# The last 64 positions of each sequence: loaded through another engine's queue, and in 9 transfers where there were 12

## The chip, the cores and the metric

The kernel runs on one core of a Trainium2 chip. A core has five engines that each work through their own list of instructions in order: TensorE (PE in the profile, with its weight loads as PEld), VectorE (DVE), ScalarE (ACT), GpSimd (POOL) and SyncE (SP). They meet only at semaphores. Sixteen DMA engines move data between the large memory and the on-chip buffers; the transfers of this kernel are issued by SyncE, and a few small ones by ScalarE. The metric is the device time of one launch in microseconds, the median of several runs.

## The reference

Two blocks follow each other, all in float32.

- Retention: q, k and v have the shape (8 batches, 8 heads, 576 positions, 64). For each batch and head the scores q·kᵀ/8 are multiplied by a causal decay, gamma_h to the power of the distance, with gamma_h = 1 − 2^(−5−h), and then multiplied with v. There is no softmax.
- The result is laid out as 4608 tokens by 512 and goes through an RMS norm with a gain, and a gated feed-forward block: silu(xn·w_gate) · (xn·w_val), and that times w_out. w_gate and w_val are 512 by 1536, w_out is 1536 by 512.

```
ret = scale * (q @ k.T) * Dmat;  x = (ret @ v) laid out as (4608, 512)
xn = x / sqrt(mean(x*x) + 1e-6) * rms_g
out = (silu(xn @ w_gate) * (xn @ w_val)) @ w_out
```

## The kernel before

**Tiling.** One job is a batch and a pair of heads; there are 32. The first 8 jobs (batches 0 and 1) are worked on in a start phase that also rounds the weights and builds sums of their blocks; the rest is one long run of matmuls on blocks of 512 tokens, in which the later jobs are placed. A sequence of 576 positions is 4 full chunks of 128 and a tail of 64. The full chunks of a job are loaded by `load_first` (line 165): one transfer for q (256 KB), two for k and two for v (128 KB each). The tails are loaded by `load_tails` (line 184), for several heads of one batch at a time, with one transfer each for q, k and v, into the tile `vi`.

**A job in the start phase.** `scale_v` (line 268, step V of the plan) multiplies v and its tail by powers of gamma, four small instructions of ScalarE. `turn` (line 222, step T) transposes q and k on TensorE, the tails too, and ScalarE copies the results out of PSUM, which gives qT and kT. `slot` (line 414, step S) then does `values` of the job before, `scores` and `states` of this one, `weigh` and `sums` on VectorE, and `carried` of the job before.

**What sets the order.** Each engine's order is the order in which the program issues work; nothing is rearranged. In `start` (line 1206) ScalarE first gets the load of its function table and one dummy activation, then three table loads (`gv`, `causal`, `gc`, line 1220). After that the list `LOADS` (line 1155) is gone through once: it holds everything that SyncE loads in this phase, in order: tails and jobs, the table `gq`, and the first halves of the weights (`load_half`, line 1031). Then the string `PLAN` (line 1134) is gone through, one step after the other; it begins with `V0 T0 a1 a1 a1 S0 T1 V1 a1 S1 T2 V2`. The tails are four entries of `LOADS` with three transfers each: heads 0 and 1 of batch 0 at the head of the list, heads 2 to 7 of batch 0 and heads 0 and 1 of batch 1 behind job 1, heads 2 to 7 of batch 1 behind job 4.

**Semaphores of the transfers.** The framework gives all transfers of SyncE and ScalarE together eight semaphores, in rotation, in the order in which it lays the transfers out. A transfer waits, in the list of the engine that issues it, until the transfer eight places before it, which had the same semaphore, has landed. So at most eight are under way. Before the change the only transfers of ScalarE are the three tables.

Of the kernel before, what the change touches and what calls it, by code (L numbers as in the profile page):

```python
# [23 lines left out]
def _decay_tables(H, D):  # L24

    pairs = _gamma(H).reshape(H // 2, 2).T
    rows = np.repeat(pairs, D, axis=0)
    pos = np.arange(L)  # L30
    p = np.concatenate([pos, pos])
    gq = rows[:, :, None] ** (pos + L) / np.sqrt(D)
    turns = np.arange(2)[None, None] * SQ + (np.arange(P) % SQ)[:, None, None] + L
    gp = rows[:, :, None] ** turns / np.sqrt(D)
    t = pairs.T[None] ** -p[:, None, None], rows**L, gq, gp
    return [np.ascontiguousarray(x).astype(np.float32) for x in t]


def _causal_table():

    return np.ascontiguousarray(np.tile(np.triu(np.ones((L, L), np.float32)), (2, 1)))
# [3 lines left out]
def kernel(  # L45
# [11 lines left out]
    nc = tc.nc  # L57
    B, H, S, D = q.shape
# [58 lines left out]
    rms_g = const.tile([P, NHP], F32, name="rms_g")  # L117
# [66 lines left out]
    def load_tails(b, heads):  # L184

        for n, (nm, src) in enumerate((("qt", q), ("kt", k), ("vt", v))):
            at = NV + (3 * b + n) * DM
            t = vi[:TAIL, at : at + DM].rearrange("p (h d) -> p h d", d=D)
            cut = slice(heads[0], heads[-1] + 1)
            nc.sync.dma_start(  # L190
                out=t[:, cut], in_=src[b, cut, NFULL * P :].rearrange("h p d -> p h d")
            )
            for hp in range(heads[0] // 2, heads[-1] // 2 + 1):
                st[b * NHP + hp][nm] = t[:, 2 * hp : 2 * hp + 2]
# [17 lines left out]
    def warm_up(n, width=P):  # L212

        if not warm_of:
            warm_of[0] = bank("warm")
        for _ in range(n):
            nc.tensor.matmul(
                warm_of[0][:, :width], lhsT=ones, rhs=ones[:, :1].to_broadcast([P, width]),
                start=True, stop=True,
            )  # L220
# [193 lines left out]
    def slot(j, rest=True):  # L414

        if rest:
            values(j - 1)
        scores(j)
        states(j)
        weigh(j)  # L420
        if j < FIRST:
            sums(j)
        if rest:
            carried(j - 1)
        if j >= FIRST:
            sums(j)
# [17 lines left out]
    def squared(u, c):  # L444
        return u, c, square(u, c)

    def gather(u, c, sq):

        if c == NHP - 1 and u > 1:
            nc.vector.scalar_tensor_tensor(  # L450
                out=sq, in0=t_of[u], scalar=EPS * DM / P, in1=sq, op0=ALU.add, op1=ALU.add
            )
        elif u < 2 and c == NHP - 1:
            sq = (t_of[u], sq)
        elif c:
            nc.vector.tensor_tensor(out=sq, in0=t_of[u], in1=sq, op=ALU.add)
        t_of[u] = sq
# [245 lines left out]
    def differences(u, f):  # L703

        hh = h_1 if u == 1 else h
        b11, b12, b22 = hh[:, f : f + 2, :HU], hh[:, f : f + 2, HU:], hh[:, NH + f : NH + f + 2, HU:]
        for o, a, b in ((t1_of(u)[:, f : f + 2], b12, b11), (b12, b22, b12)):
            nc.vector.tensor_tensor(out=o, in0=a, in1=b, op=ALU.subtract)
# [30 lines left out]
    def inner_sums(u, n, part=None, eng=nc.gpsimd):  # L739

        x = operands_of(u)[order_of(u)[n]]
        x11, x12 = x[:, :NK, :P], x[:, :NK, P:]
        x21, x22 = x[:, NK:, :P], x[:, NK:, P:]
        i1, i3, i2, i4 = inner_of(u, n)
        if part != 1:
            eng.tensor_tensor(out=i1, in0=x12, in1=x11, op=ALU.subtract)  # L746
        c = slice(1, NK) if part == 1 else slice(0, 1) if part == 0 else slice(0, NK)
        for o, a, b, op in (
            (i3, x22, x12, ALU.subtract), (i2, i3, x11, ALU.add), (i4, x21, i2, ALU.subtract),
        ):  # L750
            eng.tensor_tensor(out=o[:, c], in0=a[:, c], in1=b[:, c], op=op)  # L751
# [227 lines left out]
    def combine(b, eng=nc.vector, late=False):  # L979

        t = vec[:, b] if isinstance(b, slice) else vec[:, b : b + 1]
        for o, x, y in (
            (A12, A11, A12), (A11, A11, S2), (S1, A11, S1), (S4, S1, S4), (A11, A11, S3),
            (S3, S1, S3), (A22, A11, A22),
        ):
            eng.tensor_tensor(out=t[:, :, o], in0=t[:, :, x], in1=t[:, :, y], op=ALU.add)  # L986
        if late:
            store(NU - 1, b)
# [42 lines left out]
    def load_half(i, queue):  # L1031
        if i >= len(halves):
            return
        kind, k, a, c = halves[i]
        w = words_of(i)
        if kind == "up":
            src = (moe_w_gate, moe_w_val)[k % 2].bitcast(U32)
            n = (a * NH + k // 2 * 2) * P * 2
            src = src[2 * c * P : 2 * c * P + 2 * P, n : n + 4 * P].rearrange("(c p) f -> p c f", p=P)
            w = w.rearrange("p (c f) -> p c f", c=2)  # L1040
        else:
            f = (a * NH + c * NK + k) * P
            src = moe_w_out.bitcast(U32)[f : f + P]
        queue.dma_start(out=w, in_=src)
# [82 lines left out]
    def store_blocks(n):  # L1127

        while stores and stores[0][0] <= n:
            for o, t in stores.pop(0)[1]:  # L1130
                nc.sync.dma_start(out=o, in_=t)
# [19 lines left out]
        c0 F13 A1 v1 A1 c3 A1 j9 o0 G11 A1 A1 j10 A1 A1 j11 A1 i12 A1 R2 A1 Y2 A1 X2 M2 a1 a1  # L1151
        i13 A1 A1 A1 A1
    """
    TAILS = ((0, range(2)), (0, range(2, H)), (1, range(2)), (1, range(2, H)))
    LOADS = [("tails", 0), ("job", 0), ("job", 1), ("tails", 1), ("tails", 2), ("job", 2), ("table", 3), ("job", 3), ("half", 0), ("half", 1), ("job", 4), ("tails", 3), ("job", 5), ("job", 6), ("job", 7), ("half", 2), ("half", 3), ("rms_g", 0), ("table", 4), ("half", 4)]
    stores = []
    n_joined = 0
    due = False
# [47 lines left out]
    def start():  # L1206

        tables = list(zip((causal, gv, gc, gq, gp), (_causal_table(), *_decay_tables(H, D))))

        def table(i, queue):  # L1210
            t, values_ = tables[i]
            src = nc.inline_tensor(values_, name=t.tensor.name + "_table")
            queue.dma_start(out=t, in_=src.ap())

        make_identity(nc, ident)
        nc.scalar.activation(out=tick, in_=mhalf[:1], func=AF.Silu)
        nc.vector.memset(ones, 1.0)
        warm_up(6)
        for i in (1, 0, 2):
            table(i, nc.scalar)  # L1220
        squares, outs = [], [across(0), across(1)]
        loads = {
            "job": load_first, "table": lambda i: table(i, nc.sync),
            "half": lambda i: load_half(i, nc.sync),
            "tails": lambda i: load_tails(*TAILS[i]),
            "rms_g": lambda i: nc.sync.dma_start(
                out=rms_g, in_=moe_rms_g.rearrange("(c p) -> p c", p=P)
            ),
        }
        tasks = {  # L1230
            "S": lambda j: slot(j, rest=j not in (0, FIRST)), "C": close, "T": turn, "V": scale_v,
            "P": prepare, "F": fetch, "Q": lambda j: squares.append(squared(*divmod(j, NHP))),
            "G": lambda j: gather(*squares.pop(0)), "N": norm_1, "D": diagonals, "X": norm_2,
            "w": weights, "a": act, "d": lambda f: differences(f // 3, 2 * (f % 3)),
            "i": lambda n: inner_sums(*divmod(n, 7)),
            "j": lambda n: inner_sums(*divmod(n, 7), eng=nc.vector),
            "c": lambda b: combine(b, nc.gpsimd), "v": combine,
            "b": lambda n: (second_operand, last_operand)[n % 2](n // 2),
            "z": lambda n: store_blocks(len(halves) + 9),
            "r": refill, "W": weights_to, "A": lambda u: next(outs[u], None), "R": root_1,  # L1240
            "Y": root_2, "M": sums_of_x, "o": store,
            "k": lambda _: nc.vector.tensor_scalar(
                out=rms_k, in0=rms_g, scalar1=3.0 / 8.0 * K1, scalar2=None, op0=ALU.mult
            ), "U": lambda n: up_plain(n // 100, n // 10 % 10, n % 10),
        }
        for what, i in LOADS:
            loads[what](i)
        for step in PLAN.split():
            tasks[step[0]](int(step[1:]))

    with tc.manual_schedule():
        start()
        for u in range(2, NU):
            j0 = NHP * (u + 1)
# [60 lines left out]
```

## Time and profile before

| | |
|---|---|
| median of 3 runs | 1108.38 us (1107.13 to 1108.67) |
| the profiled execution | 1109.0 us, of which the profile's span covers 1107.2 us |
| busy share of the span | PE 98%, DVE 68%, POOL 41%, ACT 30% |
| the chain that ended last, by engine | PE 94%, DVE 2%, the rest 1% or less each |
| first step of the plan on ScalarE (V0) | begins at 8.14 us |
| first scores on TensorE (S0) | begin at 10.52 us |
| first transfer of job 0 | issued by SyncE at 2.87 us, after three transfers of tails |

Times are counted from the first instruction of the span. "SPq" and "ACTq" are the engines' sequencers, which issue transfers; their rows begin when the waits of that transfer are over. A chain row names what the end waited for, stretch by stretch. "Issue" is time in which an engine waited for nothing that the profile shows.

### The profile page before, as it was taken

How to read it: one execution, taken by the hardware profiler on the slowest of the kernel's cores; microseconds unless marked ns; L12 is line 12 of the kernel's file. 1: busy time of each engine (PE TensorE's matmuls, PEld its weight loads, DVE VectorE, ACT ScalarE, POOL GpSimd, SP SyncE). 2: the span in 40 equal slices, each digit the busy share in tenths (PEclk: the TensorE clock that was granted, in tenths of full speed). 3: DMA queues.
4: the chain of work that ended last, by engine and by line, in shares of the span. 5: the costliest groups of instructions: out<-in, count | busy, mean ns of one | idle time of the engine just before them, and what ended most of it. 6: DMA issues, size and time to landing. Idle time of an engine off the chain costs nothing.

```text
span 1107.2 us, 24479 instructions
## 1 busy us (share of the span) xinstructions
PE 1089.9 (98%) x10102; PEld 914.2 (83%) x10102; DVE 755.3 (68%) x1243; ACT 337.5 (30%) x749; POOL 458.5 (41%) x421
## 2 busy tenths in 40 slices
PE   7899999999999999999999999999999999999998
PEld 6654444479988899889988998889888998898888
DVE  4888578777866685668667775669465935594466
ACT  5745475331123411333034303331233111211110
POOL 0025335538430286026802481239311942393236
PEclk9999999999999999999999999999999999999999
DMA  8756787596878876787768865978475755585471
GB/s 203 204 174 222 262 266 218 198 339 190 288 269 225 197 262 218 207 234 231 261 197 208 284 253 160 247 232 286 146 206 199 268 200 172 183 289 162 151 249 40
DMA packets 253872, 243.60 MB, mean 220 GB/s; under 512 B 193217, under 2 KB 213825, under 8 KB 247617
## 3 DMA queue, kind: packets, MB, share of 16 engines
q1 hardware_dynamic: 252752, 241.74, 69.4%
q8 instruction: 79, 1.29, 0.5%
q10 hardware_dynamic: 1008, 0.30, 0.1%
q14 instruction: 33, 0.26, 0.1%
HBM read 211.92 MB, written 30.08 MB: 219 GB/s over the span
## 4 chain that ended last, share of the span: by engine, by line
PE 94%; DVE 2%; SPq 1%; issue 1%; DMA 1%; ACT 1%; POOL 0%; POOLq 0%; ACTq 0%; DVEq 0%
PE up L684 15%; PE x L624 13%; PE w L624 13%; PE z L624 13%; PE y L624 7%; PE xo L789 6%; PE xp L789 4%; PE zo L789 4%; PE zp L789 3%; PE yo L789 2%; PE wo L789 2%; PE av L362 2%; PE av L382 2%; PE s L292 2%; PE yp L789 2%; PE wp L789 2%
## 5 line engine op out<-in xcount | busy, mean ns | idle before, releaser
L684 PE MATMUL up<-x,ring 128*128 128x512 f32 x384 | 166.8, 594 | 0.0
L624 PE MATMUL x<-x,ring 128*128 128x256 f32 x672 | 161.0, 382 | 0.0
L624 PE MATMUL w<-sums,ring 128*128 128x256 f32 x672 | 158.9, 379 | 0.0
L624 PE MATMUL z<-x,ring 128*128 128x256 f32 x672 | 158.7, 379 | 0.0
L746 POOL TENSOR_TENSOR vi<-h 128x384 f32<-128x384 f32 x32 | 39.5, 1234 | 276.5 <-DVE h L643 267.5
L684 PEld LDWEIGHTS up<-x,ring 128*128 128x128 f32 x384 | 72.4, 190 | 88.9 <-issue 84.9
L624 PEld LDWEIGHTS z<-x,ring 128*128 128x128 f32 x672 | 127.7, 190 | 19.9 <-issue 2.9
L624 PEld LDWEIGHTS w<-sums,ring 128*128 128x128 f32 x672 | 127.6, 190 | 17.4
L624 PEld LDWEIGHTS x<-x,ring 128*128 128x128 f32 x672 | 125.4, 190 | 17.3
L751 POOL TENSOR_TENSOR vi<-h 128x384 f32<-128x384 f32 (+2 forms) x46 | 46.5, 1011 | 149.3 <-DVE h L643 149.3
L986 POOL TENSOR_TENSOR vi<-vi 128x512 f32<-128x512 f32 (+1 forms) x77 | 78.2, 1028 | 38.6 <-DVE vi L816 33.2
L624 PE MATMUL y<-sums,ring 128*128 128x256 f32 x336 | 79.4, 379 | 1.5 <-DVE sums L543 1.5
L650 ACT COPY m<-x 128x512 f32<-128x512 f32 x42 | 24.6, 586 | 174.0 <-PE x L624 174.0
L631 DVE TENSOR_TENSOR h<-u,w 128x512 f32<-128x512 f32 x42 | 28.9, 688 | 68.3 <-PE w L624 68.3
L624 PEld LDWEIGHTS y<-sums,ring 128*128 128x128 f32 x336 | 63.8, 190 | 10.5 <-issue 1.8
L631 DVE TENSOR_TENSOR u<-m,y 128x512 f32<-128x512 f32 x42 | 28.9, 688 | 63.2 <-PE y L624 62.9
L645 ACT ACTIVATE h<-h 128x512 f32<-128x512 f32 x63 | 39.7, 630 | 84.5 <-DVE h L631 84.5
L341 DVE SCALAR_TENSOR_TENSOR sum<-sum,gc,s 128x64 f32<-128x64 f32 x192 | 53.9, 281 | 6.8
L1106 POOL TENSOR_TENSOR vi<-vi 128x512 f32<-128x512 f32 (+1 forms) x24 | 40.8, 1699 | 36.8 <-DVE vi L1095 14.6
L631 DVE TENSOR_TENSOR u<-u,z 128x512 f32<-128x512 f32 x42 | 28.9, 688 | 34.7 <-PE z L624 34.7
L751 POOL TENSOR_TENSOR vi<-vi,h 128x384 f32<-128x384 f32 (+2 forms) x46 | 48.1, 1046 | 3.6
L1106 POOL TENSOR_TENSOR ring<-ring 128x512 f32<-128x512 f32 x24 | 30.6, 1278 | 42.0 <-DVE ring L1095 34.9
(311 smaller groups left out, 2068.1 us busy)
## 6 DMA issues: line engine op xcount, KB each, us to landing
ring<-w_out_blocks SPq DMA_DIRECT2D x59, 1344.0 KB, 6.6
ring<-w_up_blocks SPq DMA_DIRECT2D x42, 1792.0 KB, 7.8
w_out_blocks<-vi SPq DMA_DIRECT2D x21, 448.0 KB, 5.8
out_dram<-vi SPq DMA_DIRECT2D x64, 128.0 KB, 3.0
qraw<-in_q_dram SPq DMA_DIRECT2D x96, 72.0 KB, 4.7
kraw<-in_k_dram SPq DMA_DIRECT2D x96, 72.0 KB, 2.6
k<-in_k_dram SPq DMA_DIRECT2D x48, 128.0 KB, 2.9
v<-in_v_dram SPq DMA_DIRECT2D x48, 128.0 KB, 2.8
```

The source lines that it names most:

```text
L292: nc.tensor.matmul(s[e][side(odd), i * L : i * L + L], lhsT=d["kT"][side(e), c * L : c * L + L], rhs=d["qT"][side(e), c * L : c * L + L], ...
L341: nc.vector.scalar_tensor_tensor(out=t[:, c], in0=t[:, c - 1], scalar=gc[:, hp : hp + 1], in1=part, op0=ALU.mult, op1=ALU.add,)
L624: nc.tensor.matmul(ps[:, i * HU : i * HU + HU], lhsT=w[:, PLACE[blk], c, i * P : i * P + P], rhs=t_of[u][blk][:, c], start=(start and i == ...
L631: nc.vector.tensor_tensor(out=o, in0=a, in1=pairs_of(ps), op=ALU.add)
L645: nc.scalar.activation(out=o, in_=c, func=AF.Silu)
L650: nc.scalar.copy(out=s1, in_=pairs_of(x_))
L684: nc.tensor.matmul(ps, lhsT=w[:, PLACE[blk], c % 2, i * P : i * P + P], rhs=x_of[u][:, c], start=(c == 0), stop=(c == NHP - 1),)
L746: eng.tensor_tensor(out=i1, in0=x12, in1=x11, op=ALU.subtract)
L751: eng.tensor_tensor(out=o[:, c], in0=a[:, c], in1=b[:, c], op=op)
L789: nc.tensor.matmul(ps, lhsT=lhs[:, c], rhs=w[:, s, c], start=((nm, s // 4) not in first), stop=False, skip_group_check=True,)
L986: eng.tensor_tensor(out=t[:, :, o], in0=t[:, :, x], in1=t[:, :, y], op=ALU.add)
L1106: nc.gpsimd.tensor_tensor(out=t[o], in0=t[x], in1=t[y], op=op)
```

## The change

`load_tails` issues on ScalarE's queue. The tails leave `LOADS`; they are loaded in `start` between and behind the three tables that ScalarE loads already: the tails of heads 0 and 1 of batch 0 behind `gv`, those of heads 2 to 7 of batch 0 and of all heads of batch 1 behind `gc`. The two entries for batch 1 become one, so that there are 9 transfers instead of 12, with the same bytes. Everything else is as it was; lines below `start`'s head move by up to three.

```
@@ in load_tails
-            nc.sync.dma_start(
+            nc.scalar.dma_start(
                 out=t[:, cut], in_=src[b, cut, NFULL * P :].rearrange("h p d -> p h d")
             )
@@ beside the plan
-    TAILS = ((0, range(2)), (0, range(2, H)), (1, range(2)), (1, range(2, H)))
-    LOADS = [("tails", 0), ("job", 0), ("job", 1), ("tails", 1), ("tails", 2), ("job", 2), ("table", 3), ("job", 3), ("half", 0), ("half", 1), ("job", 4), ("tails", 3), ("job", 5), ("job", 6), ("job", 7), ("half", 2), ("half", 3), ("rms_g", 0), ("table", 4), ("half", 4)]
+    TAILS = (0, range(2)), (0, range(2, H)), (1, range(H))
+    LOADS = [("job", 0), ("job", 1), ("job", 2), ("table", 3), ("job", 3), ("half", 0), ("half", 1), ("job", 4), ("job", 5), ("job", 6), ("job", 7), ("half", 2), ("half", 3), ("rms_g", 0), ("table", 4), ("half", 4)]
@@ in start
-        for i in (1, 0, 2):
-            table(i, nc.scalar)
+        table(1, nc.scalar)
+        load_tails(*TAILS[0])
+        table(0, nc.scalar)
+        table(2, nc.scalar)
+        for heads in TAILS[1:]:
+            load_tails(*heads)
@@ the loads by name
-            "tails": lambda i: load_tails(*TAILS[i]),
```

## The prediction

> **What bounds the kernel now.** I read the page's first part, then the chain of waits over the first 80 us, then ScalarE's timeline at the start, then the table of stretches. The page:
>
> ```profile
> span 1107.2 us, 24479 instructions
> PE 1089.9 (98%) x10102; PEld 914.2 (83%) x10102; DVE 755.3 (68%) x1243; ACT 337.5 (30%) x749; POOL 458.5 (41%) x421
> ```
>
> TensorE is busy 98% of the span. From 60 us on its idle time is 3.9 us in all, and every piece of it that the waits name is a wait on work that itself follows from TensorE's. A microsecond lost or won ahead of that run goes into the time whole. The change lies in the first 30 us, so I read the chain there (start, length, what):
>
> ```profile
> 2.22 0.61 SPq L190
> 2.83 0.04 issue
> 2.87 2.87 DMA h<-in_q_dram
> 5.74 0.02 issue
> 5.76 0.42 SPq L172
> ...
> 12.14 0.61 SPq L190
> 12.74 0.04 issue
> 12.79 0.96 SPq L172
> ...
> 14.30 4.99 DMA h<-in_k_dram
> 19.29 0.04 issue
> 19.33 0.67 PE turn_k L230 x4
> ```
>
> Up to 19.3 us the end hangs on SyncE's list: three tails (L190) stand before job 0's q, six more stand between 8.56 and 12.79, and TensorE then waits for job 2's k until 19.33. Line 5.76 shows something else: SyncE's next transfer begins 0.02 us after one has landed. That is the rotation of eight semaphores at work. From 20 us on the chain is nearly all TensorE's. ScalarE in the same stretch:
>
> ```profile
> 1.80 0.45 ACTq L1213 DMA_DIRECT2D gc<-gc_table  x1
> ...
> 8.14 0.51 ACT L273 ACTIVATE h<-h,gv 128x256 f32<-128x256 f32 x1 [5.92 <-DMA h<-in_v_dram]
> ...
> 9.43 0.56 ACT L241 COPY qT<-turn_q 128x512 f32<-128x512 f32 x1
> ...
> 10.48 0.21 ACT L252 COPY kT<-turn_t 128x64 f32<-128x64 f32 x1
> ```
>
> It is free from 2.25 on, V0 begins when v of job 0 has landed, and the first scores on TensorE begin at 10.52, that is 2.4 us after V0 began.
>
> **What the Trainium skill says.** "DMA: Bandwidth & Descriptors", section "Issuing engines are not separate DMA queues": transfers from several engines share the same 16 DMA engines, and a second issuing engine saves only sequencer time. The trace agrees as far as it goes: a tail's issue occupies SyncE for 0.60 to 0.88 us. "Perfetto Trace Analysis", section "DMA Instruction — HWDGE (DVE, Sync)": the wait for semaphores is the sequencer's, and a row starts when it is over. The row at 5.76 agrees. So a waiting transfer on ScalarE holds up all that ScalarE does behind it. "TensorE: Matmul & The Clock Gate", section "Part 1: The HAM clock gate (the "warmup" mystery)": after an idle window of about 3.4 us the clock is halved, and about 3.4 us of sustained work restore it. The trace fits, in a stretch of few and thin matmuls (last but two columns: clock):
>
> ```profile
> 45.00:50.00 5.00, 4.66 (x131) 4.33 (x122) 4.61 (x14) 2.55 (x8) 0.85 (x2) 1.00 0.97 320
> 50.00:55.00 5.00, 3.90 (x14) 2.22 (x14) 3.07 (x8) 4.51 (x12) 0.26 (x1) 0.57 0.58 152
> 55.00:60.00 5.00, 5.00 (x143) 3.98 (x143) 4.21 (x9) 1.66 (x3) 0.09 (x1) 0.75 0.82 142
> ```
>
> **Part 1: SyncE's list gets shorter by 12 issues.** Three before job 0: 0.77 + 0.62 + 0.61 with the gaps, 2.14 us. Six before job 2: 12.79 − 8.56 = 4.23 us. Three before job 5: from 26.52 to 29.82, 3.3 us. What can be earned is the wait for job 2's k, 1.34 us of idle TensorE before 19.33; I count **−1.3 us**. Job 0 arriving 2.1 us earlier would be worth as much if ScalarE could use it (part 2). The later loads hide behind TensorE's work already; earlier is worth nothing there.
>
> **Part 2: ScalarE's list gets longer by 9 issues, all ahead of V0.** On ScalarE the order is now gv, three tails, causal, gc, six tails, and only then V0, T0's four copies, and so S0. Issue time alone: nine at about 0.65 us (L190 rows) and three tables at 0.36 to 0.45, from 0.93: about 8.5 us with the gaps. But each of them also waits for the transfer that had its semaphore before, and the built program says which:
>
> ```
> ACT: v tail (heads 0,1)   after q of job 0 has landed
>      causal               after k, first half, of job 0
>      gc                   after gv
>      q tail (heads 2-7)   after q tail (heads 0,1)
>      k tail (heads 2-7)   after v, second half, of job 0
>      v tail (heads 2-7)   after causal
>      q tail (batch 1)     after q tail (heads 2-7)
>      k tail (batch 1)     after k tail (heads 2-7)
>      v tail (batch 1)     after v, second half, of job 1
> SP:  q of job 1           after k, second half, of job 0
>      v, 2nd half, job 1   after q of job 1
> ```
>
> I walk this with times to landing that the trace of before has: 256 KB of q 2.9 (alone) to 3.7 us, 128 KB of k and v 2.7 to 3.6, tails 2.3 to 3.4, tables 1.6 to 2.2; in a full queue one more 128 KB per 0.45 to 0.5 us. All results are estimates.
>
> - q of job 0 is issued at 0.73 and lands at 3.6; its k at 4.1 and 5.0, its v at 5.5 and 6.0.
> - ScalarE: q and k tails at 1.3 and 2.0, v tail at 3.6, causal at 4.2, gc at 4.7, q tail at 5.2, k tail at 6.1 (v of job 0), v tail at 6.8 (causal landed).
> - q tail of batch 1 waits for the one issued at 5.2: 5.2 + 3.4 = 8.6. The k tail follows at 9.5.
> - SyncE: q of job 1 waits until 5.0 and lands at 8.6; the second half of v waits for that and lands at 8.6 + 3.4 = 12.0.
> - So the last v tail is issued at 12.0 and ScalarE is free at **12.7**. With all landings at their short end it is 11.0, with all at the long end 13.9.
>
> V0 then begins 12.7 − 8.14 = **4.6 us** later than before (2.9 to 5.8), with its data long there, and S0 at about 15.1 instead of 10.52. TensorE, which has turned job 0 by about 6.5, stands still for 8 us. No other work covers this: VectorE waits for S0 too. What is late next: everything; the steps to S1 took 3.6 us of engine work and stay. Job 2's k, issued at about 10.5 and landed by 14.5, is no longer waited for at 24.
>
> **Part 3: the clock.** Before, TensorE had no pause of over 2 us in this stretch. A pause of 8 us holds more than one window of 3.4 us, so S0 should start at half clock. The first turn of q, 16 matmuls on a TensorE that had just started, took 1.97 us, the second 1.09; turn_k took 1.12 and 0.66. One window of 3.4 us at such a rate does some 1.7 us less work. Bounds: 0 (the copies on ScalarE and the sums on VectorE set the pace) and 3.4 (two windows). I take **+1.7**.
>
> **Part 4: at nothing.** The merging of 12 into 9 saves three issues, which are in part 1. Bytes are the same. Later tails are needed first by job 1's turn at about 18, job 4's at 33; they land by 10 and by 15.5. TensorE's pauses named "issue" between 25 and 51 (0.40, 0.71, 1.55, 0.51, 1.44: 4.6 us) each end 2.3 to 3.0 us after a packet of the instruction queue begins, so they are fetches that share the DMA engines with loads. With the loads further ahead of the work they may shrink, with other overlaps grow: −1.5 to +1, taken as 0.
>
> **Sum.** −1.3 + 4.6 + 1.7 = +5.0 us on the span of 1107.2, so 1112.2. The profiled execution took 1109.0, 1.8 above its span; the median of the runs is 1108.38, 0.6 below that. On the median: 1108.4 + 5.0 = **1113.4 us**.
>
> **Rivals.** About 0.2% (2.2 us) is what a measurement of this kernel can tell from no change.
>
> - *Not slower: ScalarE isn't held.* If the landings come early enough that the semaphores hardly bind, only the issue time counts: free at 8.8, V0 0.7 later, the wait for job 2 gone, no long pause: 1108.4 + 0.7 − 1.3 = 1107.8. The deciding point is ScalarE free at 9.5; up to there it isn't slower, and up to about 11.7 with a warm clock it can't be told apart. Against it: the chain has two landings of loaded transfers in a row behind q of job 1, which can't start before job 0's k. 0.08.
> - *Offset later.* The half clock of 50 to 58 us (PE at 0.57 in the stretch above) falls away because other work lies in that window. The scores there took 0.84 us against 0.58, the two norm matmuls 2.00 against 0.86: worth some 3 us. With a fetch of 1.4 less: 1113.4 − 4.4 = 1109.0. For it: it is one window's accident; against: the thin matmuls that bring it about remain. 0.09.
> - *Worse.* Landings at the long end (+1.2) and two windows at half clock (+1.7): 1116.3. 0.13.
> - *As forecast:* 0.70, with 1111 to 1115.5 as its own range.
>
> **How the numbers follow.** Slower by over 0.2%: the forecast, the worse case, and a third of the offset, 0.70 + 0.13 + 0.03, taken as 0.85. Within 0.2%: the rest of the offset and half of the first rival, 0.11. Faster: 0.04. The range 1109.8 to 1117.0 leaves out the first rival and about half of the offset below, and the far end of the worse case above.
>
> **What would show it.** ScalarE's V0 begins between 11 and 14 us, right behind the issue of the last v tail; that issue starts right after a landing of job 1's v; TensorE idles from about 6.5 to 15; the clock is below 1 after it; no wait for job 2's k; the rest of the trace moved by 3 to 6 us. I am wrong if V0 begins before 10 us, if S0's matmuls run at full rate, or if the pauses and the half clock between 25 and 58 us add up otherwise than before.

## The result and the profile after

| | median us | lowest to highest | runs |
|---|---|---|---|
| before | 1106.78 | 1105.70 to 1109.18 | 11 |
| after | 1111.56 | 1109.69 to 1114.51 | 11 |

The changed kernel takes 1.0037 times as long, with an interval of 1.0026 to 1.0048: some 4 us more (2.9 to 5.3). The profiled execution of after took 1111.3 us, 1109.5 of them in the span. That is 2.3 us above the profiled execution of before; the medians differ by 4.8. The two figures don't contradict each other, and why they differ is part of what follows. (One correction to the description of the reference: the weights come as 64-bit floats and are rounded in the start phase. This concerns neither the change nor the times.)

The page of after, span and busy shares:

```profile
span 1109.5 us, 24470 instructions
PE 1086.7 (98%) x10102; PEld 912.8 (82%) x10102; DVE 756.5 (68%) x1243; ACT 337.3 (30%) x749; POOL 458.1 (41%) x421
```

It tells nothing: TensorE's share is the same, and even its busy time is lower. The answer lies in the first 16 us. ScalarE's timeline of after (start, length, engine and line, operation; in brackets the idle time of the compute part before it, and what ended it):

```profile
3.52 0.60 ACTq L190 DMA_DIRECT2D vi<-in_v_dram  x1
4.16 0.61 ACTq L1213 DMA_DIRECT2D causal<-causal_table  x1
...
7.10 0.64 ACTq L190 DMA_DIRECT2D vi<-in_v_dram  x1
9.22 0.60 ACTq L190 DMA_DIRECT2D vi<-in_q_dram  x1
10.48 0.65 ACTq L190 DMA_DIRECT2D vi<-in_k_dram  x1
12.70 0.60 ACTq L190 DMA_DIRECT2D vi<-in_v_dram  x1
13.35 0.51 ACT L273 ACTIVATE h<-h,gv 128x256 f32<-128x256 f32 x1 [11.13 <-DMA h<-in_q_dram]
```

The rows of L190 are the tails. The last three are batch 1's, and between them ScalarE issues nothing and computes nothing: 7.74 to 9.22, 9.82 to 10.48, 11.13 to 12.70. V0 (L273) comes 0.05 us behind the last of them, at 13.35 instead of 8.14. The bracket names a transfer of q as the last thing awaited; the rows above it show what it really was, the place in ScalarE's list. The second half of job 1's v was issued at 8.85 and took 3.8 us to land, until 12.68, and the last tail is issued 0.02 us later. In the trace both carry the same semaphore (number 105): that is the transfer whose semaphore the tail had to have. SyncE's timeline, and the time to landing of that one transfer:

```profile
8.85 0.37 SPq L180 DMA_DIRECT2D h<-in_v_dram  x1
```

```profile
h<-in_v_dram SPq DMA_DIRECT2D x1, 128.0 KB, 3.8
```

TensorE's timeline in the same stretch has a pause of 8.5 us, and the table of stretches (its last three columns are granted clock, DMA share and GB/s) shows the clock at half through most of it and still low behind it. First the scores of S0 in before, then in after, then the stretches of after:

```profile
10.52 0.81 PE L292 MATMUL s<-qT,kT 64*64 64x64 f32 x40 [0.37 <-ACT kT L241]
```

```profile
15.74 1.35 PE L292 MATMUL s<-qT,kT 64*64 64x64 f32 x40 [8.50 <-ACT kT L241]
```

```profile
10.00:15.00 5.00, 0.00 (x0) 0.00 (x0) 0.00 (x0) 1.65 (x5) 0.00 (x0) 0.50 1.10 263
15.00:20.00 5.00, 4.26 (x93) 3.81 (x93) 2.52 (x8) 1.37 (x5) 0.00 (x0) 0.60 1.10 272
...
50.00:55.00 5.00, 4.85 (x161) 4.71 (x160) 4.75 (x15) 2.50 (x10) 0.09 (x1) 1.00 0.01 5
55.00:60.00 5.00, 4.02 (x110) 2.78 (x108) 3.75 (x11) 4.93 (x14) 1.11 (x2) 1.00 0.30 79
```

The last two rows hold the surprise. Between 50 and 60 us the clock is full, where before it was at 0.57 and 0.75. So I cut both spans at four places: V0 begins on ScalarE, S0 and S2 begin on TensorE, and the first matmul of the feed-forward part (L684, "U0" here) begins.

| | before | after | difference |
|---|---|---|---|
| span's start to V0 | 8.14 | 13.35 | +5.2 |
| V0 to S0 | 2.38 | 2.39 | 0.0 |
| S0 to S2 | 10.20 | 10.23 | 0.0 |
| S2 to U0 | 38.43 | 35.41 | −3.0 |
| U0 to the end | 1048.1 | 1048.1 | 0.0 |
| span | 1107.2 | 1109.5 | +2.3 |

5.2 us are lost ahead of S0 and 3.0 are won between 26 and 61 us, where the code is the same. The experiments had to settle two things: what holds V0, and whether the 3.0 us are the change's own.

### The profile page after: what moved, and what is told of

Read it like the earlier page. It is cut to its first block, busy times and chain, and to the rows that moved or that the text cites. A ratio compares the mean times of both kernels' runs of the same rounds, so it can differ in the third digit from the quotient of the medians.

```text
span 1109.5 us, 24470 instructions
## 1 busy us (share of the span) xinstructions
PE 1086.7 (98%) x10102; PEld 912.8 (82%) x10102; DVE 756.5 (68%) x1243; ACT 337.3 (30%) x749; POOL 458.1 (41%) x421
## 4 chain that ended last, share of the span: by engine, by line
PE 94%; DVE 2%; ACT 1%; DMA 1%; issue 1%; POOL 0%; SPq 0%; POOLq 0%; ACTq 0%; DVEq 0%
PE up L684 15%; PE x L624 13%; PE w L624 13%; PE z L624 13%; PE y L624 7%; PE xo L789 6%; PE xp L789 4%; PE zo L789 4%; PE zp L789 3%; PE yo L789 2%; PE wo L789 2%; PE av L362 2%; PE av L382 2%; PE s L292 2%; PE yp L789 2%; PE wp L789 2%
## 5 line engine op out<-in xcount | busy, mean ns | idle before, releaser
L684 PE MATMUL up<-x,ring 128*128 128x512 f32 x384 | 166.8, 594 | 0.0
L684 PEld LDWEIGHTS up<-x,ring 128*128 128x128 f32 x384 | 72.4, 190 | 88.9 <-issue 85.1
L624 PEld LDWEIGHTS x<-x,ring 128*128 128x128 f32 x672 | 125.4, 190 | 17.3
L1106 POOL TENSOR_TENSOR vi<-vi 128x512 f32<-128x512 f32 (+1 forms) x24 | 40.6, 1694 | 36.9 <-DVE vi L1095 14.6
L325 DVE SCALAR_TENSOR_TENSOR ret<-s,causal 128x320 f32<-128x320 f32 x64 | 28.7, 484 | 29.2 <-PE s L292 28.2
```

The source lines that it names most:

```text
L325: nc.vector.scalar_tensor_tensor(out=ret[:, e], in0=s[e][:, : n * L].rearrange("p (c k) -> p c k", k=L), scalar=float(_gamma(H)[2 * hp + e ...
L624: nc.tensor.matmul(ps[:, i * HU : i * HU + HU], lhsT=w[:, PLACE[blk], c, i * P : i * P + P], rhs=t_of[u][blk][:, c], start=(start and i == ...
L684: nc.tensor.matmul(ps, lhsT=w[:, PLACE[blk], c % 2, i * P : i * P + P], rhs=x_of[u][:, c], start=(c == 0), stop=(c == NHP - 1),)
L1106: nc.gpsimd.tensor_tensor(out=t[o], in0=t[x], in1=t[y], op=op)
```

## The experiments

Two theories of the held V0. A: ScalarE is held by the *waits* of the transfers in its list; most of the loss comes from the three tails of batch 1, whose semaphores belong to late transfers. B: it is the *number* of transfers ahead of V0, or the tails' own landing. For the second half of the phase: either the change moves the pauses and the clock in a settled way, or they are chance that differs between any two executions. Ratios are to the kernel before, with a 95% interval; the medians of before that was run beside them are 1106.7 to 1107.3.

**1 and 2: three or six tails on ScalarE.** The rest goes back to SyncE, in the first run heads 2 to 7 behind job 1 and batch 1 behind job 3, in the second only batch 1 behind job 3.

```
d3_act, against after
-    def load_tails(b, heads):
+    def load_tails(b, heads, queue=nc.scalar):
     LOADS = ... ("job", 1), ("tails", 1), ("job", 2), ("table", 3), ("job", 3), ("tails", 2), ("half", 0), ...
-        for heads in TAILS[1:]:
-            load_tails(*heads)
+            "tails": lambda i: load_tails(*TAILS[i], nc.sync),
d6_act: the same, but load_tails(*TAILS[1]) stays on ScalarE and ("tails", 1) is not in LOADS
```

> Only the three tails of heads 0 and 1 of batch 0 stay on ScalarE; heads 2 to 7 go back to SyncE behind job 1, batch 1 (one set of three) to SyncE behind job 3. Theory A (ScalarE is held by landings that its later tails wait for): its list ends at about 5.3 us, V0 begins when job 0's v has landed, about 6.5, S0 at 8.9, 1.6 us before the kernel before. SyncE has six issues fewer ahead of job 2, about 4 us, so there is no wait for job 2's k, another 1.3 us. Sum -2.9 us: about 1103.9 where the kernel before takes 1106.8. Theory B (each tail on ScalarE costs its issue time, and so in proportion): a third of the loss, about +1.5 us to the kernel before.

> Six tails on ScalarE (batch 0), batch 1 on SyncE behind job 3. Theory A: the sixth is issued at 7.1 as in the changed kernel, V0 begins at about 7.8, S0 at 10.2 (0.3 us before the kernel before), no wait for job 2's k: -1.6 us, about 1105.1; the three left out were worth 5.6 us of delay of V0. Theory B: the three left out are worth their issue time, 1.9 us, so V0 at 11.4 and S0 at 13.8: about +2 to +3 us.

Measured: d3_act 1105.57 us, ratio 0.9983 (0.9974 to 0.9993); d6_act 1106.26 us, 0.9993 (0.9984 to 1.0003). ScalarE's timeline of d6_act:

```profile
6.43 0.60 ACTq L190 DMA_DIRECT2D vi<-in_k_dram  x1
7.07 0.64 ACTq L190 DMA_DIRECT2D vi<-in_v_dram  x1
7.76 0.51 ACT L273 ACTIVATE h<-h,gv 128x256 f32<-128x256 f32 x1 [5.54 <-DMA gc<-gc_table]
```

V0 begins at 7.76 with six tails and at 13.35 with nine. The three that make the difference take 0.60 + 0.65 + 0.60 = 1.85 us to issue and cost 5.6. Theory B has no room for that. (The time itself came out 1.0 us lower than before, where I had expected 1.6, and its interval includes no change.) With three tails V0 begins at 5.71, when its own data have landed:

```profile
4.80 0.44 ACTq L1213 DMA_DIRECT2D gc<-gc_table  x1
5.71 0.51 ACT L273 ACTIVATE h<-h,gv 128x256 f32<-128x256 f32 x1 [3.49 <-DMA vi<-in_v_dram]
```

So loading the *first* tails from ScalarE is a gain, 2.4 us at V0. In the median of d3_act 1.7 us arrive (1107.25 to 1105.57). One reason stands in its chain of waits: job 4's q, pushed back by the three tails behind job 3, is now late.

```profile
21.98 5.64 DMA ring<-in_q_dram
27.62 0.14 issue
27.76 0.62 PE turn_q L236 x6
```

**3: six later tails behind T0 in ScalarE's list.** If the waits hold ScalarE, the hold should move to wherever the tails stand.

```
-        for heads in TAILS[1:]:
-            load_tails(*heads)
+            "L": lambda i: load_tails(*TAILS[i]),
-        V0 T0 a1 a1 a1 S0 T1 V1 ...
+        V0 T0 L1 L2 a1 a1 a1 S0 T1 V1 ...
```

> The changed kernel with the six later tails behind the plan's step T0 in ScalarE's list, not ahead of V0. Theory A (ScalarE is held wherever the tails stand): V0 at 5.7 and S0 at 8.4 as with three on ScalarE; then the six are issued, the last one after a landing at about 16.5 to 17.5 us, and T1's copies, which need ScalarE, begin only then and not at about 11: S1 at 18 to 19.5. Sum: 1 to 3 us slower than the kernel before, 1 to 3 faster than the changed one. Rival (only what stands ahead of V0 counts, or the order of the loads): S1 by 13.5, and 2 us faster than the kernel before.

Measured: 1111.74 us, 1.0045 (1.0028 to 1.0061). Its ScalarE timeline:

```profile
8.38 0.21 ACT L252 COPY kT<-turn_t 128x64 f32<-128x64 f32 x1
8.56 0.67 ACTq L190 DMA_DIRECT2D vi<-in_q_dram  x1
10.81 0.60 ACTq L190 DMA_DIRECT2D vi<-in_k_dram  x1
15.23 0.60 ACTq L190 DMA_DIRECT2D vi<-in_v_dram  x1
...
17.95 0.60 ACTq L190 DMA_DIRECT2D vi<-in_v_dram  x1
18.60 0.58 ACT L241 COPY qT<-turn_q 128x512 f32<-128x512 f32 x1 [10.01 <-DMA vi<-in_v_dram]
```

The hold went along: V0 at 5.86, S0 at 8.43, as in d3_act, and then ScalarE does no work for 10 us until the last tail is issued. S1 begins at 19.72 (20.79 in after). The last tail went out at 17.95, somewhat later than expected (16.5 to 17.5), but the hold stands where it was to stand. The total was some 2 us and more above what I had expected, and this profile has half clock in two stretches, 13.7 to 24.0 and 37.6 to 41.0.

**4: all nine tails on GpSimd's queue.** GpSimd has little to do in the first 20 us, so nothing waits behind its transfers.

```
-            nc.scalar.dma_start(
+            nc.gpsimd.dma_start(
```

> The nine tails on GpSimd's queue, ScalarE with its three tables alone. Theory A: V0 at about 6.5, S0 at 8.9, no wait for job 2's k: -2.9 us to the kernel before, about 1103.9. Rival: issues from GpSimd take over 1 us each and land late, job 0's tails hold up the turn, and job 1's too: up to +2 us.

Measured: 1106.24 us, 0.9992 (0.9982 to 1.0002). GpSimd's timeline:

```profile
1.47 0.77 POOL L190 DMA_DIRECT2D vi<-in_q_dram  x1 [0.16 <-issue]
...
6.67 0.70 POOL L190 DMA_DIRECT2D vi<-in_v_dram  x1
```

The nine are issued one after the other, 0.59 to 0.77 us each, and held by nothing. V0 begins at 6.56, S0 at 8.95, as expected. The loss of the change is gone, with the same bytes in the same number of transfers, so neither the number of the tails nor their bytes make it. The run doesn't separate two things, though: nothing stands behind the tails in GpSimd's list, and they don't have to wait, since the trace shows GpSimd's transfers with eight semaphores of their own. That work behind a waiting transfer is held is what late6 shows. S0 is 1.6 us earlier than before, and the median 1.0 us lower (1107.25 to 1106.24), where I had expected 2.9; the interval can't quite tell it from none.

**5: a mixture.** Three tails on ScalarE, three on GpSimd at the start, and batch 1's on GpSimd behind S1.

```
+        load_tails(*TAILS[1], nc.gpsimd)      # in place of the loop
-        ... S0 T1 V1 a1 S1 T2 V2 ...
+        ... S0 T1 V1 a1 S1 L2 T2 V2 ...       # L: load_tails on nc.gpsimd
```

> Three tails (heads 0 and 1 of batch 0) on ScalarE, heads 2 to 7 of batch 0 on GpSimd at the start, batch 1 on GpSimd behind the plan's step S1. Nothing of the tails on SyncE, nothing that waits for a late landing on ScalarE. S0 at 8.4 as with three on ScalarE, S1 3.6 to 4.6 later (no wait for job 1's tails), no wait for the loads of jobs 2 and 4: 3 us before the kernel before at S2. If pauses for instructions grow no more than in the runs so far, 2 to 3 us faster than the kernel before, about 1104.5; if they eat it as with nine on GpSimd, 1106.

Measured: 1109.0 us, 1.0016 (1.0003 to 1.0029): a miss, slower than before instead of faster. ScalarE's timeline and the chain:

```profile
4.82 0.44 ACTq L1213 DMA_DIRECT2D gc<-gc_table  x1
7.32 0.51 ACT L273 ACTIVATE h<-h,gv 128x256 f32<-128x256 f32 x1 [5.08 <-DMA h<-in_v_dram]
```

```profile
3.53 4.43 DMA vi<-in_v_dram
7.98 0.35 ACT vi L273
```

With three queues issuing at once job 0's v tail was under way for 4.43 us and landed at 7.96 (d3_act, two queues: by 6.4), and V0 waited for job 0's v, until 7.32. That explains 1.6 us of S0 against d3_act. It does not explain why the median lies 2.3 us above that of before although S0 begins earlier than there (9.97); S2 to U0 took 37.2 us in the one profile, which is not out of the ordinary, and this profiled execution (1107.6 us) is itself 1.4 below the median. This stays open.

**6: the merging alone.** Before, with batch 1's tails in 3 transfers instead of 6, all on SyncE.

```
-    TAILS = ((0, range(2)), (0, range(2, H)), (1, range(2)), (1, range(2, H)))
+    TAILS = ((0, range(2)), (0, range(2, H)), (1, range(H)))
-    LOADS = ... ("job", 4), ("tails", 3), ("job", 5), ...
+    LOADS = ... ("job", 4), ("job", 5), ...
```

> The kernel before with the tails of batch 1 in one set of three transfers on SyncE, at the place of the first of its two sets: 9 transfers, all on SyncE. Theory A: merging alone is worth nothing that can be measured; the wait for job 2's k stays or grows by some tenths, since the merged set stands before job 2: within 1 us of the kernel before. Rival: fewer issues are what counts, 1 to 2 us faster.

Measured: 1106.66 us, 1.0003 (0.9989 to 1.0017). Twelve transfers into nine is worth nothing that can be told from no change.

**7: the kernel before once more**, unchanged, for a second profile.

> The kernel before once more, for a second profile: V0 at 8.1, S0 at 10.5, the wait for job 2's k of about 1.3 us again. If the half clock between 50 and 58 us belongs to the kernel it is there again; if it depends on where the clock's windows fall it is elsewhere or gone, and the span then shorter by about 3 us.

It took 1109.65 us, with a span of 1107.9. Chain and table of stretches:

```profile
10.51 1.35 PE s L292 x40
...
12.71 1.93 PE turn_q L236 x16
```

```profile
10.00:15.00 5.00, 4.86 (x93) 4.00 (x92) 2.71 (x9) 1.01 (x4) 0.00 (x0) 0.54 0.58 138
```

S0 begins at 10.51 (10.52), but the clock is at half from 7.7 to 14.6 and from 28.2 to 31.6, and full between 50 and 58, where the first profile had it at half. S0's scores took 1.35 us, as long as in after, and S0 to S1 5.4 us instead of 3.6. There is no wait for job 2's k. Its second half, the one that TensorE had waited for, took 2.7 us from its issue at 14.61:

```profile
h<-in_k_dram SPq DMA_DIRECT2D x1, 128.0 KB, 2.7
```

So it landed at 17.3, in the first profile at 19.29, after 4.99 us. There TensorE had come to it at 17.99: at full clock too it would have found this k landed. And S2 to U0 took 38.3 us all the same, with 4.8 us of "issue" pauses. So where the half clock lies is not a property of the kernel.

**8: the clock after the pause.** After, with 16 dummy matmuls instead of one in job 0's turn, which keep TensorE busy while it waits.

```
-        warm_up(j == 0, 2 * P)
+        warm_up(16 * (j == 0), 2 * P)
```

> The changed kernel with 16 dummy matmuls of 256 columns, not 1, behind job 0's turn, to keep TensorE busy while ScalarE is held; their result is not used. Theory A with the clock: V0 stays at 13.3, S0 at about 15.7 but at full clock, S0 to S1 takes 3.6 us and not 5.0: 1.4 us less than the changed kernel, about 1110.2. Rival: the half clock costs nothing, because copies and sums set the pace: same as the changed kernel, 1111.6.

Measured: 1113.8 us, 1.0058 (1.004 to 1.0076). The gain that I had expected (1110.2) is not there; whether the kernel is slower than after can't be told, since the intervals overlap (1.0026 to 1.0048 for after). The chain of waits:

```profile
14.66 0.81 PE s L292 x40
15.94 1.05 PE turn_q L236 x16
...
23.53 1.16 issue
...
27.86 2.06 issue
...
56.57 2.07 PE rb L529 x2
```

The local part came as expected: S0's scores take 0.81 us instead of 1.35, and S0 to S1 takes 3.61 us instead of 5.05. (S0 itself is 1.1 us earlier because the second half of job 1's v landed earlier, at 11.6.) Then two new pauses stand at 23.5 and 27.9, the clock is at half from 30.4 to 33.8, and again from 54.3 to 61.1; S2 to U0 takes 37.5 us instead of 35.4. Beside after, the 2.7 us of the span add up so: S0 −1.1, S0 to S1 −1.4, S1 to S2 +1.4, S2 to U0 +2.1, the rest +1.7. What the full clock gave, the next stretches took back, the first of them by the pause at 23.5.

**9: more DMA traffic where TensorE's next instructions are fetched.** After, with four copies of 512 KB from memory to memory behind job 7's loads and the next weights; nothing uses them. The last load of weights in `LOADS` (`half` 4) comes behind them. Lines move down by six in this kernel: L298 is L292 elsewhere.

```
+        for i in range(4):
+            t = dram.tile([256, 512], U32, name=f"extra_{i}")
+            nc.sync.dma_start(out=t, in_=moe_w_val.bitcast(U32)[:256, 512 * i : 512 * i + 512])
```

> The changed kernel with four additional copies of 512 KB each from memory to memory, issued by SyncE behind the loads of job 7, so that the DMA engines are busy between 40 and 50 us where they idle in the changed kernel. Nothing waits for the copies. If TensorE's pauses named issue are instruction fetches that stand behind data transfers, there is at least one more such pause after 42 us (none in the changed kernel), 1 to 3 us in sum, and the first matmul of the feed-forward part (61.4 us) comes that much later. If they belong to places in the program, nothing changes.

Measured: 1114.85 us, 1.0074 (1.005 to 1.0099). Chain and table of stretches:

```profile
44.08 0.58 PE s L298 x37
44.67 2.90 issue
47.56 0.37 PE s L298
```

```profile
40.00:45.00 5.00, 4.27 (x126) 3.66 (x126) 4.25 (x12) 2.45 (x8) 0.09 (x1) 1.00 1.02 352
45.00:50.00 5.00, 2.44 (x60) 2.44 (x62) 2.42 (x8) 2.52 (x8) 0.00 (x0) 0.73 0.77 263
```

In after the same stretches have 27 and 107 GB/s, the instruction queue's packets that begin at 42.6 and 46.5 us leave no trace, and TensorE doesn't pause. Here TensorE stands for 2.90 us, and the clock is at half from 47.3 to 50.7. The packet that ends the pause begins only at 45.17, 0.5 us after TensorE has stopped and 7.0 us after the packet before it (3.6 us in after), and takes 1.06 us itself, no longer than many others. So the fetch was late in starting, and what held it back in the full DMA engines isn't shown. U0 comes 2.7 us later although S0 was 0.95 us earlier. This is what I had expected if DMA load at the time of a fetch makes these pauses. One profile doesn't prove it: fill16 and late6, without the copies, have pauses after 42 us too (1.20 and 0.56, 0.59 us), though none so long. That the other pauses named "issue" have this cause is inferred from their like timing. The Trainium skill, "Runtime: NRT & Kernel Launch", section "Instruction fetch mechanics", says that the sequencer fetches its instructions in blocks through a DMA queue of its own, and that crossing a block costs little that isn't hidden. The first half agrees (the profile of after has 79 packets on a queue of that kind). The second does not where the DMA engines are busy: 2.90 us here, 1.21 and 2.39 in after.

**10: d3_act with another order of loads.** Batch 1's tails and the second half of the first weight move behind job 4.

```
     LOADS = ... ("job", 3), ("half", 0), ("job", 4), ("tails", 2), ("half", 1), ("job", 5), ...
```

> Three tails on ScalarE as in d3_act, and on SyncE the tails of batch 1 and the second half of the first weights behind job 4, not ahead of it. In d3_act TensorE waited 1.9 us for q of job 4 at 27.8, where it lands at 27.6; now it lands about 4 us earlier. Up to 1.9 us faster than d3_act, if no pause for instructions takes its place: 1103.5 to 1105.5.

Measured: 1104.99 us, 0.9985 (0.9972 to 0.9997). The wait for job 4's q is gone; of TensorE's idle time ahead of job 4's turn only 1.0 us named "issue" is left. Against d3_act the difference is within the error. Both are faster than either kernel of this case: three tails at the head of ScalarE's list, the rest with SyncE.

Over all profiles, the stretch from S2 to U0, in which the code of all these kernels is the same but for the places of some loads (us; pauses named "issue" of 0.2 us or more on the chain of waits, and time at half clock, within the stretch):

| | S0 | S2 | S2 to U0 | "issue" | half clock | U0 to end |
|---|---|---|---|---|---|---|
| before | 10.52 | 20.72 | 38.4 | 4.6 | 6.8 | 1048.1 |
| before, second profile | 10.51 | 21.11 | 38.3 | 4.8 | 3.4 | 1048.4 |
| after | 15.74 | 25.97 | 35.4 | 3.6 | 0 | 1048.1 |
| d3_act | 8.40 | 18.38 | 37.0 | 0.5 | 6.8 | 1048.2 |
| d6_act | 10.14 | 20.32 | 36.4 | 5.0 | 0 | 1048.1 |
| late6 | 8.43 | 26.24 | 35.0 | 3.1 | 3.4 | 1048.9 |
| pool9 | 8.95 | 18.91 | 36.2 | 4.2 | 0 | 1047.9 |
| mix | 9.97 | 20.31 | 37.2 | 4.4 | 3.4 | 1048.3 |
| merge_sp | 10.22 | 21.01 | 39.0 | 4.1 | 6.8 | 1047.9 |
| fill16 | 14.66 | 24.86 | 37.5 | 3.8 | 10.2 | 1049.8 |
| extra4 | 14.79 | 25.85 | 38.2 | 5.9 | 3.4 | 1048.2 |
| d3_order | 8.52 | 18.31 | 37.2 | 1.7 | 3.4 | 1047.9 |

The stretch lasts 35.0 to 39.0 us. The three profiles without half clock have 35.4 to 36.4, the nine with it 35.0 to 39.0, most of them over 37. So half clock goes with the longer stretches, but the table alone doesn't make it their cause, and not each value follows from these two columns (late6 has half clock and the shortest stretch; d3_act has the wait for job 4's q on top).

## Why the prediction was right

Forecast was 1113.4 us against a median of 1108.4, +5.0; measured are +4.8 between the medians of 11 runs each, and +4.1 (2.9 to 5.3) as the ratio. The kernel before came out 1.6 us lower than in its first three runs, and with it the absolute time. The mechanism of the loss was right; that the sum came so near is in part luck, since misses in its terms offset each other. Step by step:

- **Part 2, ScalarE's list, +4.6.** Right in mechanism and nearly in size. ScalarE was free at 13.3 instead of 12.7, inside the bounds of 11.0 and 13.9; V0 moved by 5.2, S0 with it. The walk of semaphores named the last link: the last tail behind the second half of job 1's v, landed at 12.68 instead of 12.0. The 5.2 belong to this one profile: fill16 and extra4, whose code is the same up to here on ScalarE and SyncE, have V0 at 12.27 and 12.41, 4.1 and 4.3 behind before. d6_act shows that batch 1's tails hold V0 by 5.6 us, late6 that the hold goes where they go, pool9 that nine tails which neither wait nor stand ahead of other work cost nothing.
- **Part 3, the clock, +1.7.** S0 began at half clock; S0 to S1 took 5.05 us instead of 3.61, +1.4. fill16, which keeps the clock up, has 3.61 there.
- **Part 1, job 2's k, −1.3.** The wait is gone, S1 to S2 is 1.4 shorter. But the reading behind it was wrong in part: I had put the wait down to the six tails in SyncE's list. The second profile of before has the same list and no wait, because its k took 2.7 us to land and not 4.99. So the wait came of one slow landing (why it was slow isn't shown), and the earlier issue in after, landed by 14.8, only makes room for it. Nor is the half clock at S0 the change's own to the full; the second profile of before has it, too. S0 to S2 took 10.2 us in before, 10.6 in its second profile and 10.2 in after. fill16 has full clock at S0 and no wait for k, and still took 6.6 us from S1 to S2, 1.2 of them a pause named "issue". I had added −1.3 and +1.7, to +0.4; measured is 0.0, by two sums of different parts that happen to be equal.
- **Part 4, "at nothing".** This is the step that failed, and by the prediction's own sign: the pauses and the half clock between 25 and 58 us added up otherwise than before. The merging is worth nothing (merge_sp), but S2 to U0 was 3.0 us shorter in the profile of after than in that of before. The "issue" pauses are 1.0 of it, inside the −1.5 to +1 that I had given them. The rest I had left out of this step: the half clock at 50 to 58 us, which is missing in after. That is the rival "offset later", and in the two profiles it took place. But it is not a settled gain of the change: the stretch took 35 to 39 us in the twelve profiles, half clock came and went in it, in before too, and fill16 and extra4 show how little is needed to bring it back. In the medians little of it is left: +4.8, or +4.1 by the ratio, against 4.1 to 5.2 for V0 in the three profiles. With the ratio's whole interval up to 2.3 us could be left, so that a smaller gain of the change in this stretch is not ruled out. The profiled execution of before lies 2.2 us above the median of its 11 runs, that of after 0.2 below; this is where the 2.3 us of the profiles and the 4.8 of the medians part. That a run of before at the median has less half clock in this stretch than the profiled one is an inference from the clocks of many runs (below), not seen in a trace. So +4.6 and +0.4 came near the right sum, and the −3 that would have spoilt it is, as far as these runs tell, mostly what one execution differs by from another.
- **The rivals.** "ScalarE isn't held" is refuted by its own deciding point: ScalarE was free at 13.3, not by 9.5. "Worse" would have needed 1116.3.

Not tried: more than eight semaphores in rotation, which would leave the tails on ScalarE and take their waits away. The framework sets the number.

## What to carry to other kernels

A transfer issued by an engine that also computes holds that engine's computing for as long as the *transfer* has to wait, and with semaphores in rotation that is the landing of a transfer eight places before it, perhaps another engine's. Put on such an engine only what can be issued before its first real work, ask of each of them whose landing it waits for, and leave the rest with an engine that has no work of its own behind it. And where differences of 2 us are at stake, take a second profile of the kernel before: what looked like the change's gain in one stretch lay within what two executions differ by.

## What I had not expected of the hardware

- **The granted clock splits the executions of one unchanged kernel.** Of 119 executions of the kernel before in three sets, the 32 with a mean granted clock of 0.9985 or more have a median of 1104.7 us, the 63 at about 0.997 and 0.998 1107.3, the 24 at 0.996 or less 1108.9. The changed kernel's 11 runs all lie at 0.994 to 0.997, and the 10.2 us at half clock around its long pause make 0.995 by themselves. The Trainium skill, "TensorE: Matmul & The Clock Gate", section "Part 1: The HAM clock gate (the "warmup" mystery)", describes the clock in windows of about 3.4 us; the stretches at half clock here are 3.4, 6.8 and 10.2 us long, one, two and three windows.
- **TensorE stood for up to 2.9 us at an instruction fetch** in busy DMA traffic (extra4). Of the 36 pauses named "issue" of 0.2 us or more that the chains of the twelve profiles have between S2 and U0, all but two ended 2.2 to 3.0 us after a packet of an instruction queue had begun.
- **Whether such a pause costs clock on top goes with where it falls.** The steps of the clock in one trace are whole multiples of 3.41 us apart, so its windows can be laid over the trace. extra4's pause of 2.90 us (44.67 to 47.56) lies almost whole in one window; TensorE is busy in it for 0.81 us (first column behind the comma), and the next window is at half clock:

```profile
43.86:47.27 3.41, 0.81 (x52) 0.67 (x43) 2.04 (x4) 3.41 (x11) 0.09 (x1) 1.00 1.02 353
47.27:50.69 3.42, 3.12 (x67) 3.01 (x69) 1.84 (x7) 0.25 (x1) 0.00 (x0) 0.50 0.46 161
```

After's pause of 2.39 us (38.77 to 41.16) is cut by a border at 39.45, and the clock stays:

```profile
36.03:39.45 3.42, 2.74 (x118) 2.36 (x117) 1.92 (x7) 3.32 (x7) 0.09 (x1) 1.00 1.00 336
39.45:42.86 3.41, 1.70 (x41) 1.64 (x43) 2.41 (x9) 0.12 (x1) 0.00 (x0) 1.00 0.28 94
42.86:46.27 3.41, 3.04 (x92) 2.34 (x88) 3.03 (x7) 2.96 (x9) 0.09 (x1) 1.00 0.00 0
```

In the twelve profiles half clock sets in 11 times between S2 and U0: nine times behind a window in which TensorE was busy for 54% or less of the time, twice behind one with 70 and 83% (before at 50.7, fill16 at 54.3). It is no sharp limit: five windows with 46 to 54% were followed by full clock.

- **GpSimd issued these transfers as fast as SyncE and ScalarE**: 0.59 to 0.77 us each, against 0.60 to 0.88 for SyncE's tails before.
- **A third queue isn't free for the first transfers**: with SyncE, ScalarE and GpSimd issuing at once (mix) job 0's v tail took 4.43 us from issue to landing, and V0 began 1.6 us later than with two. Whether the third queue does it or the three transfers more that are under way at once isn't separated.
